# Sliding attention and squared-ReLU MLP, gated: the first tile of tokens in one transfer, four token tiles in turn, warm-up products on the program's constant zero

## The chip, the cores and the metric

The kernel runs on one core of one Trainium2 chip. The core has a matrix engine (TensorE, PE in the profile; its loads of the stationary operand are listed apart as PEld), a vector engine (VectorE, DVE), a scalar engine (ScalarE, ACT), GpSimd (POOL) and a queue engine (SyncE, SP) from which this kernel issues all its transfers. Times are device microseconds of one execution. The metric is the median over several executions; lower is better.

## The reference, cut to what matters

Two branches read the same 2048 tokens of width 448 and are mixed by a gate per token.

```python
g = sigmoid((x * gate_w).sum(-1, keepdims=True))
# branch a: q, k, v for 16 heads of 28; each token sees 8 keys, 2 apart, behind it
qkv = x @ wqkv                                   # 448 -> 3*448
logits = einsum("bhsd,bhswd->bhsw", q, k[idx]) * 28 ** -0.5   # idx = pos - 2*(0..7), masked below 0
o = einsum("bhsw,bhswd->bhsd", softmax(logits), v[idx])
a = o.reshape(1, 2048, 448) @ wo
# branch b: MLP with a squared ReLU
h = relu(x @ w1 + b1) ** 2                       # 448 -> 1792
b = h @ w2 + b2
out = g * a + (1 - g) * b
```

Everything is float32. The kernel splits each operand of a product into a high part in a 32-bit format that TensorE takes at full pace, and a low part, which is the rest. Three products, high by high, high by low and low by high, then stand for one float32 product.

## The kernel before, in words

The tokens lie in four chunks of 512 columns, each of four tiles of 128 tokens; even tokens are in the first two chunks, odd ones in the last two. The width of 448 is cut into three blocks of 128 rows and a last one of 64. These blocks are called k = 0, 1, 2, 3 below, and the last is kept twice, in both halves of the partitions, so that two products of 64 rows run side by side.

The order of the work on every engine is written out by hand. A running estimate of TensorE's time, `advance`, only decides when an operation of another engine is emitted in between; `at` and `when` hang such operations onto that clock. An engine takes its instructions strictly in the order in which they were emitted.

The phases on TensorE are: warm-up products (line 632), which multiply zeros and whose results nobody reads; the query, key and value products of chunk 0 in `qkv_first`; those of chunks 1 to 3 in `qkv_two`, with the first MLP products mixed in; then the MLP of all four chunks, with the output products of attention between them. Attention itself runs on GpSimd and VectorE beside the MLP, by way of copies in HBM.

The first stretch is the one that concerns us. All transfers are issued from SP, in this order: for each k the weights of the query block (line 639 for k below 3, two issues in line 642 for k = 3), then the block of tokens, `rx` (line 644; in the profile `xraw`), which for k = 0 goes in two transfers of 256 columns each; then the key and value weights (lines 649 and 652), then chunk 1 (line 565). SP's transfers pass through eight semaphores in turn, so that a transfer also waits for the one eight places ahead of it.

For each k below 3, ScalarE makes the high part of the weights (line 655) and of the tokens in two halves (line 662). The very first half, k = 0, is made by VectorE instead (line 660). VectorE then makes the low part of the weights (line 663) and those of the two halves of the tokens (line 665). `split_full` (lines 114 and 115) does the same for k = 3.

`qkv_first` makes four accumulators of queries, one for each token tile. For each k it takes the token tiles 0 and 1 first, with three products each (high by high, low weights, low tokens), in turn between the two tiles, and then tiles 2 and 3 in the same way (line 266). Tiles 0 and 1 lie in the first half of the columns, 2 and 3 in the second half. The side-by-side products of k = 3 and all that follows go through `side_by_side` (line 188).

The warm-up products read `zero`, a tile of 128 x 256 which VectorE clears (line 629); it takes a turn in the ring of four product buffers `pp`. Line 630 clears `none`, one element of `b1z`, which ScalarE reads later. The program also has a constant zero of its own, one column of 128 elements, which GpSimd writes before the engines start on the kernel's own instructions (in the profile `const-float32-0.0`).

Of the kernel before, what the change touches and what calls it, by code (L numbers as in the profile page):

```python
# [7 lines left out]
F32 = mybir.dt.float32  # L8
F32R = mybir.dt.float32r
# [5 lines left out]
P = 128  # L15
# [7 lines left out]
CH = 512  # L23
NQ = D + 2
# [23 lines left out]
LEAD = 5  # L48
DEFER = 2
ORDER = (3, 0, 1, 2)  # L50
WARM = 13
PP_BUFS = 4
ST_BUFS = 3
BT_BUFS = 8
# [3 lines left out]
def gated_mix_kernel(ctx: ExitStack, tc: tile.TileContext, xT, wqkv, w1, w2, wo, b1, b2, out):  # L58
    nc = tc.nc

    def f32(ap):
        return ap.bitcast(F32)
# [31 lines left out]
    prodp = ctx.enter_context(tc.tile_pool(name="prodp", bufs=1))  # L94
# [73 lines left out]
    def block(b):  # L168

        o = (0, NP, NP + D)[b]  # L170
        return slice(o, o + ncols(b))
# [45 lines left out]
    def full(x, acc, tl, b, ks=range(3)):  # L217
        sl, n = slice(tl * P, tl * P + P), block(b)
        r = []
        for k in ks:  # L220
            r += [(acc, x.h[k][:, sl], wqh[:, k, n]), (acc, x.h[k][:, sl], wql[:, k, n]),
                  (acc, x.l[k][:, sl], wqh[:, k, n])]
        return r
# [33 lines left out]
    def qkv_first(x):  # L257


        four = range(4)  # L260
        q = accs(0, 0, four, "bbbb")
        for k in range(3):
            for two in ((0, 1), (2, 3)):
                for j, prods in enumerate(zip(*(full(x, q[i], i, 0, (k,)) for i in two))):
                    for acc, a, w in prods:
                        nc.tensor.matmul(acc.pt[:, :NQ], a, w, start=k == j == 0, stop=False)  # L266
            advance(12 * MM448)
        for acc in q:
            acc.todo = 3
        k = accs(0, 1, four, "mmmm")  # L270
        t = [sum((last(x, a[i], i, b) for i in four), []) for b, a in ((0, q), (1, k))]
        f = [full(x, k[i], i, 1) for i in four]
        run(0, [t[0] + f[0] + f[1] + f[2] + f[3], t[1] + f[2] + f[3] + f[0] + f[1]],
            [(3, [(0, 0, q[0])], (k[0], k[0])),
             (12, [(0, i, q[i]) for i in (1, 2, 3)], (k[1], k[1])),
             (24, [], (k[0], k[2])), (33, [], (k[1], k[3])),
             (39, [(1, 0, k[0]), (1, 2, k[2])]), (48, [(1, 1, k[1]), (1, 3, k[3])])])
        v = accs(0, 2, four, "bbbb")
        f, l = [full(x, v[i], i, 2) for i in four], [last(x, v[i], i, 2) for i in four]
        run(0, [f[0] + l[0] + f[2] + l[2] + f[1] + f[3], f[1] + l[1] + f[3] + l[3] + f[0] + f[2]],  # L280
            [(15, [], (v[0], v[1])), (24, [], (v[2], v[3])),
             (33, [(2, 0, v[0]), (2, 1, v[1])]), (42, [(2, 2, v[2]), (2, 3, v[3])])])
# [342 lines left out]


    warm = ps("m", "warm")
    zero = prodp.tile([P, 2 * P], F32R, tag="pp", name="zero", bufs=PP_BUFS)
    nc.vector.memset(f32(zero), 0.0)  # L629
    nc.vector.memset(none, 0.0)  # L630
    for _ in range(WARM):
        nc.tensor.matmul(warm[:, :2 * P], zero[:, :P], zero, start=True, stop=True)  # L632
# [3 lines left out]
    rx = raw_tile("xraw0")  # L636
    for k in range(4):
        if k < 3:
            nc.sync.dma_start(raws[0][:, k, :NQ], wqkv[0, :, k])
        else:  # L640
            for b, rows in ((0, slice(0, 64)), (1, slice(64, P))):
                nc.sync.dma_start(raws[0][rows, k, :NQ], wqkv[b, rows, k])
        for cols in ((slice(0, 256), slice(256, CH)) if k == 0 else (slice(0, CH),)):
            nc.sync.dma_start(rx[:, k, cols], xT[0, :, k, cols])

    for b, tag in ((1, "k"), (2, "v")):
        raw = attp.tile([P, 3, D], F32, tag=tag, name=f"wqraw{b}")
# [5 lines left out]
    x = x_tiles(0, xap)  # L653
# [93 lines left out]
    for c in range(4):  # L747
        x = xs[c]
# [291 lines left out]
    c, x = ORDER[0], xm[3]  # L1040
# [8 lines left out]
    for g in range(2, 2 * NF):  # L1049
        i, f = g // (NF // 2), g % (NF // 2) * 2  # L1050
# [4 lines left out]
        if not f:  # L1055
            x, slots = X([nxt[j][0] for j in range(4)]), [nxt[j][1] for j in range(4)]
# [113 lines left out]
```

## Time and profile before

| | us |
|---|---|
| median of 3 runs | 415.18 |
| lowest and highest run | 414.21, 415.46 |
| the profiled execution | 414.58 |
| its span, first to last instruction | 412.7 |
| TensorE busy (share of the span) | 408.4 (99%) |
| GpSimd busy | 268.6 (65%) |
| VectorE busy | 255.9 (62%) |
| ScalarE busy | 211.9 (51%) |
| DMA of SP's queue, share of 16 engines' span | 54.5% |

The profile is that of one execution. Its rows give the start of a group in microseconds from the start of the span, the time from its first start to its last end, the engine, the line of the kernel, the operation, what it writes and reads, and how many instructions are merged; in brackets stands the idle time before it and what ended that. A row of SPq is the issuing of a transfer and not the transfer itself. Matrix products are pipelined: one product's row is longer than the distance to the next one's start, so that the distance between starts is what tells the pace.

### The profile page before, as it was taken

What the parts mean: (1) busy time and instruction counts of PE and PEld (TensorE: products, weight loads), DVE (VectorE), ACT (ScalarE), POOL (GpSimd) and SP (SyncE); (2) the same over time, 40 slices, a digit from 0 to 9 for tenths busy, and PEclk for the clock granted to TensorE, in tenths of its full rate; (3) what the DMA queues carried; (4) which work ended last, traced back from release to release, by engine and by line L of the source; (5) the groups of instructions that cost most, each with busy time, mean ns of one, the idle gap of its engine ahead of it and who ended that gap; (6) DMA issues with size and microseconds to landing.
All of it is one profiled execution on the core that took longest, in us unless ns stands there. A gap on an engine that the chain in (4) does not pass through costs nothing.

```text
span 412.7 us, 9323 instructions
## 1 busy us (share of the span) xinstructions
PE 408.4 (99%) x3835; PEld 377.6 (91%) x3835; DVE 255.9 (62%) x404; ACT 211.9 (51%) x477; POOL 268.6 (65%) x167
## 2 busy tenths in 40 slices
PE   8999999999999999999999999999999999999997
PEld 8999999999999999888888888989898888888996
DVE  4520523276767767777656798879576677892354
ACT  5642556378756565444565535444653254346540
POOL 0000000965989999999989899999899977860000
PEclk9999999999999999999999999999999999999999
DMA  7989799989164307654112649765145611168204
GB/s 236 380 318 326 227 364 292 363 259 321 47 224 159 128 2 258 207 186 152 37 50 93 233 157 266 200 149 149 24 163 192 224 46 59 72 175 139 91 0 180
DMA packets 65611, 73.76 MB, mean 179 GB/s; under 512 B 32352, under 2 KB 58528, under 8 KB 65184
## 3 DMA queue, kind: packets, MB, share of 16 engines
q1 hardware_dynamic: 65568, 73.16, 54.5%
q8 instruction: 30, 0.49, 0.5%
q14 instruction: 13, 0.11, 0.1%
HBM read 45.71 MB, written 28.25 MB: 179 GB/s over the span
## 4 chain that ended last, share of the span: by engine, by line
PE 99%; DVE 0%; issue 0%
PE b L188 33%; PE h L188 32%; PE qkv L188 23%; PE a L188 7%; PE qkv L266 2%; PE warm L632 1%; PE a L944 1%; PE last L944 0%; DVE bt L823 0%; PE last L936 0%; PE a L936 0%; DVE zero L629 0%; DVE b1z L630 0%
## 5 line engine op out<-in xcount | busy, mean ns | idle before, releaser
L339 POOL TENSOR_TENSOR qk<-q,k 128x896 f32<-128x896 f32 x64 | 135.0, 2138 | 83.2 <-DMA k<-k_d 78.9
L346 POOL TENSOR_TENSOR av<-lg,v 128x896 f32<-128x896 f32 x64 | 119.5, 1962 | 8.0 <-DVE lg L340 5.6
L188 PE MATMUL qkv<-wqh,x 64*128 64x448 f32 (+1 forms) x528 | 90.9, 360 | 0.0
L619 DVE TENSOR_TENSOR h<-h,h 128x512 fp32r<-128x512 f32 x56 | 38.3, 687 | 60.8 <-ACT h L622 60.4
L188 PEld LDWEIGHTS qkv<-wqh,x 64*128 64x128 f32 x528 | 74.0, 184 | 1.3
L188 PE MATMUL qkv<-wql,x 64*128 64x448 f32 (+1 forms) x264 | 74.7, 360 | 0.0
L188 PE MATMUL b<-w2ah,h 64*128 64x448 f32 x448 | 70.4, 359 | 0.0
L188 PE MATMUL b<-w2bh,h 64*128 64x448 f32 x448 | 69.6, 360 | 0.0
L340 DVE TENSOR_REDUCE lg<-qk 128x32 f32<-128x896 f32 x64 | 67.1, 1076 | 2.2 <-POOL qk L339 2.1
L354 DVE TENSOR_REDUCE o<-av 128x112 f32<-128x896 f32 x64 | 66.5, 1070 | 2.1 <-POOL av L346 1.8
L620 ACT ACTIVATE h<-h,b1z 128x512 f32<-128x512 f32 x56 | 36.7, 656 | 44.0 <-PE h L188 44.0
L188 PEld LDWEIGHTS b<-w2ah,h 64*128 64x128 f32 x448 | 48.0, 184 | 2.8
L188 PEld LDWEIGHTS b<-w2bh,h 64*128 64x128 f32 x448 | 46.0, 184 | 3.2 <-ACT h L571 0.3
L188 PE MATMUL b<-w2al,h 64*128 64x448 f32 x224 | 47.6, 358 | 0.0
L188 PEld LDWEIGHTS qkv<-wql,x 64*128 64x128 f32 x264 | 45.5, 184 | 0.7
L188 PE MATMUL b<-w2bl,h 64*128 64x448 f32 x224 | 45.8, 358 | 0.0
L207 ACT ACTIVATE st<-qkv 128x448 f32<-128x448 f32 x48 | 24.5, 543 | 32.2 <-PE qkv L188 27.1
L188 PE MATMUL h<-x,w1h 64*128 64x512 f32 x168 | 36.1, 386 | 0.0
L621 ACT ACTIVATE h<-h 128x512 fp32r<-128x512 f32 x56 | 33.5, 599 | 1.7
L622 ACT ACTIVATE h<-h 128x512 f32<-128x512 f32 x56 | 33.2, 593 | 0.0
L188 PE MATMUL h<-x,w1l 64*128 64x512 f32 x84 | 29.7, 386 | 0.0
L571 ACT ACTIVATE h<-h 128x4 fp32r<-128x4 f32 (+1 forms) x35 | 7.2, 206 | 42.6 <-PE b L188 42.4
(145 smaller groups left out, 749.4 us busy)
## 6 DMA issues: line engine op xcount, KB each, us to landing
k<-k_d SPq DMA_DIRECT2D x8, 840.0 KB, 6.7
v<-v_d SPq DMA_DIRECT2D x8, 840.0 KB, 4.4
x_d<-x SPq DMA_DIRECT2D x11, 512.0 KB, 6.0
q_d<-st SPq DMA_DIRECT2D x8, 448.0 KB, 4.6
k_d<-st SPq DMA_DIRECT2D x8, 448.0 KB, 4.1
v_d<-st SPq DMA_DIRECT2D x8, 448.0 KB, 7.1
w1raw<-w SPq DMA_DIRECT2D x4, 896.0 KB, 10.0
q<-q_d SPq DMA_DIRECT2D x8, 448.0 KB, 3.6
```

Of the source, the lines that this page charges most:

```text
L188: nc.tensor.matmul(acc.pt[:, :acc.n], a[rows], w[rows], start=acc.todo == acc.all, stop=acc.todo == 1)
L207: nc.scalar.activation(st[:, :, t % 2], pt[:, :D].rearrange("p (g c) -> p g c", g=G), AF.Copy)
L266: nc.tensor.matmul(acc.pt[:, :NQ], a, w, start=k == j == 0, stop=False)
L339: nc.gpsimd.tensor_mul(pr, q[:, s:s + 1].to_broadcast([P, W, C]), k[:, s:s + W])
L340: pending.append(lambda: nc.vector.tensor_reduce(lg[:, s], pr.rearrange("p w (h d) -> p w h d", h=HG), axis=AX.X, op=ALU.add))
L346: nc.gpsimd.tensor_mul(pr.rearrange("p (h d) w -> p w h d", h=HG), lg[:, s][:, :, :, None].to_broadcast([P, W, HG, DH]), v[:, s:s + W].rea ...
L354: nc.vector.tensor_reduce(o[:, g * C:(g + 1) * C], pr, axis=AX.X, op=ALU.add)
L571: nc.scalar.activation(ap, f32(ap), AF.Copy)
L619: nc.vector.tensor_sub(hl, pt, f32(hh))
L620: ops += [lambda pt=pt, r=r: nc.scalar.activation(pt, pt, AF.Relu, bias=b1t[:, f + r:f + r + 1]), lambda pt=pt, hh=hh: nc.scalar.activatio ...
L621: lambda pt=pt, hh=hh: nc.scalar.activation(hh, pt, AF.Square),
L622: lambda pt=pt, r=r, low=low: (nc.scalar.activation(pt, pt, AF.Square), at(delays[r], low))]
```

## The change

Four edits. The warm-up products read the program's constant zero, one column repeated 128 and 256 times, and the tile `zero` with its clearing is gone. There are 16 of them where there were 13. The first block of tokens (k = 0) is loaded by one transfer of 512 columns instead of two of 256. `qkv_first` takes all four token tiles in turn for each kind of product: four times high by high, four times low weights, four times low tokens. The splitting of the tokens on ScalarE and VectorE still goes by halves, and nothing else in the program is reordered.

```diff
-WARM = 13
+WARM = 16
@@ qkv_first
         for k in range(3):
-            for two in ((0, 1), (2, 3)):
-                for j, prods in enumerate(zip(*(full(x, q[i], i, 0, (k,)) for i in two))):
-                    for acc, a, w in prods:
-                        nc.tensor.matmul(acc.pt[:, :NQ], a, w, start=k == j == 0, stop=False)
+            for j, prods in enumerate(zip(*(full(x, q[i], i, 0, (k,)) for i in four))):
+                for acc, a, w in prods:
+                    nc.tensor.matmul(acc.pt[:, :NQ], a, w, start=k == j == 0, stop=False)
             advance(12 * MM448)
@@ warm-up
-    zero = prodp.tile([P, 2 * P], F32R, tag="pp", name="zero", bufs=PP_BUFS)
-    nc.vector.memset(f32(zero), 0.0)
+    zero = nc.const_aps.tensor(0.0, [P, 2 * P], F32).bitcast(F32R)
     nc.vector.memset(none, 0.0)
     for _ in range(WARM):
         nc.tensor.matmul(warm[:, :2 * P], zero[:, :P], zero, start=True, stop=True)
@@ first loads
-        for cols in ((slice(0, 256), slice(256, CH)) if k == 0 else (slice(0, CH),)):
-            nc.sync.dma_start(rx[:, k, cols], xT[0, :, k, cols])
+        nc.sync.dma_start(rx[:, k], xT[0, :, k])
```

## The prediction

> **What bounds the kernel now.** I read the page's busy shares, slices and chain first, then the busy time by stretch, then the waits of TensorE, then the timeline of the first 13 us.
>
> ```profile
> PE 408.4 (99%) x3835; PEld 377.6 (91%) x3835; DVE 255.9 (62%) x404; ACT 211.9 (51%) x477; POOL 268.6 (65%) x167
> PE   8999999999999999999999999999999999999997
> PEclk9999999999999999999999999999999999999999
> PE 99%; DVE 0%; issue 0%
> ```
>
> TensorE is busy for 99% of the span and the chain that ended last runs on it for 99%. The next view is the busy time of each engine in four stretches (start:end, length, then PE, PEld, DVE, ACT, POOL, clock, DMA share, GB/s).
>
> ```profile
> 0.00:13.00 13.00, 11.80 (x53) 10.83 (x54) 7.42 (x17) 7.57 (x14) 0.81 (x13) 1.00 0.81 267
> 13.00:100.00 87.00, 87.00 (x866) 84.93 (x864) 31.73 (x97) 49.31 (x118) 19.25 (x10) 1.00 0.93 316
> 100.00:405.00 305.00, 305.00 (x2894) 277.84 (x2892) 213.83 (x287) 154.99 (x346) 248.50 (x145) 1.00 0.43 136
> 405.00:412.70 7.70, 4.62 (x34) 4.02 (x30) 2.91 (x6) 0.00 (x0) 0.00 (x0) 1.00 0.51 184
> ```
>
> From 13 to 405 us TensorE shows 392.00 us busy of 392.00. No wait there can absorb a shift of the first stretch, and none shows that could be shortened. The edit touches the first stretch alone, and what moves the end of that stretch moves the end of the kernel one for one. TensorE has one long wait, at the very start:
>
> ```profile
> PE warm L632 <- DVE b1z L630: 1.2, 1, 1.2
> ```
>
> **The first 13 us.** The timeline (start, length, engine, line, operation, count):
>
> ```profile
> 0.24 0.10 POOL L1162 MEMSET const-float32-0.0<- 128x1 f32 x1 [0.24 <-issue]
> 0.74 1.28 ACT L655 ACT_TABLE_LOAD   x1 [0.74 <-PEq L1162]
> 0.75 0.39 SPq L639 DMA_DIRECT2D wqraw<-wqkv  x1
> 0.87 0.27 DVE L629 MEMSET zero<- 128x256 f32 x1 [0.87 <-PEq L1162]
> 1.08 0.06 DVE L630 MEMSET b1z<- 1x1 f32 x1
> 1.20 3.14 PE L632 MATMUL warm<-zero 128*128 128x256 f32 x13 [1.20 <-DVE b1z L630]
> 1.20 0.89 SPq L644 DMA_DIRECT2D xraw<-xT  x2
> 2.13 0.43 SPq L639 DMA_DIRECT2D wqraw<-wqkv  x1
> 4.13 1.03 PE L266 MATMUL qkv<-wqh,x 128*128 128x450 f32 x2
> 4.96 0.95 PE L266 MATMUL qkv<-wql,x 128*128 128x450 f32 x2
> 5.71 1.44 PE L266 MATMUL qkv<-wqh,x 128*128 128x450 f32 x4
> 6.99 0.57 PE L266 MATMUL qkv<-wql,x 128*128 128x450 f32 x2
> 7.39 0.96 PE L266 MATMUL qkv<-wqh,x 128*128 128x450 f32 x4
> 12.20 0.56 PE L266 MATMUL qkv<-wqh,x 128*128 128x450 f32 x2
> 12.69 0.47 PE L188 MATMUL qkv<-w7h,x 64*128 64x450 f32 x2
> ```
>
> The starts, not the lengths, give the pace. A product of L266 comes every (5.71 - 4.96)/2 = 0.375 us at first, and from 7.39 to 12.20 every 4.81/24 = 0.200 us. TensorE runs at about half speed until somewhere in the group at 5.71, although the granted clock reads full in every slice. Of that group's four, taking 6.99 - 5.71 = 1.28 us, a at 0.375 and 4 - a at 0.200 give a = 2.74: the clock opened at 5.71 + 2.74 x 0.375 = **6.74**, which is 5.54 us after the first warm-up product.
>
> So the stretch has three numbers: S, the start of the first real product (4.13); g, the opening (6.74); and 36 products of L266. The first costs 0.08 extra (0.83 us for two, against 0.75). Then (6.74 - 4.21)/0.375 = 6.75 products run slowly and 29.25 x 0.200 = 5.85 us follow, to 12.59; 0.10 more goes at the switch to L188 at 12.69. A microsecond on S costs 0.200/0.375 = 0.53 us at the end, one on g costs 0.47.
>
> The data that these products need:
>
> ```profile
> 3.34 0.58 ACT L655 ACTIVATE wqh<-wqraw 128x450 fp32r<-128x450 f32 x1 [1.31 <-DMA wqraw<-wqkv]
> 3.64 0.29 DVE L660 CAST x<-xraw 128x256 fp32r<-128x256 f32 x1 [2.50 <-DMA xraw<-xT]
> 3.95 0.63 DVE L663 TENSOR_TENSOR wql<-wqraw,wqh 128x450 fp32r<-128x450 f32 x1
> 4.49 0.42 DVE L665 TENSOR_TENSOR x<-xraw,x 128x256 fp32r<-128x256 f32 x1
> 5.54 0.42 ACT L662 ACTIVATE x<-xraw 128x256 fp32r<-128x256 f32 x1 [1.63 <-DMA xraw<-xT]
> 6.18 0.58 ACT L655 ACTIVATE wqh<-wqraw 128x450 fp32r<-128x450 f32 x1 [0.23 <-DMA wqraw<-wqkv]
> 6.93 0.72 ACT L662 ACTIVATE x<-xraw 128x256 fp32r<-128x256 f32 x2 [0.17 <-DMA xraw<-xT]
> 8.86 0.72 ACT L662 ACTIVATE x<-xraw 128x256 fp32r<-128x256 f32 x2 [0.73 <-DMA xraw<-xT]
> 2.00:3.00 1.00, 1.00 (x6) 1.00 (x6) 0.00 (x0) 0.03 (x1) 0.00 (x0) 1.00 0.84 284
> ```
>
> **The change, part by part.**
>
> *Warm-up operand.* The clear of 0.27 us on DVE goes, and with it TensorE's wait for DVE. The constant zero is written at 0.24 to 0.34, ahead of the first instruction of every queue at about 0.74. TensorE can start between 0.74 (ACT) and 0.87 (DVE); I take the middle, 0.80, a gain of 0.40 us. At worst it stays at 1.20. The clear of b1z stays on DVE, with nothing in front; its reader is ten microseconds away. A ring of four product buffers loses one early owner, POOL's first product comes late in the 13 to 100 stretch: nothing.
>
> *Sixteen warm-ups.* Thirteen took 4.13 - 1.20 = 2.93 us, 0.225 each; sixteen take 3.61. They end at 0.80 + 3.61 = **4.41** instead of 4.13, which costs 0.28 on S if the data are there earlier. That a column read over and over goes at the pace of a tile is not shown; the nearest rows are these thirteen products, and I take their pace.
>
> *One transfer for the first x tile.* L644 issues two for it now, in 0.89 us. One goes, so the queue behind it (weights of the second tile, then x, and so on) moves up by about 0.44 us, the third transfer from 2.13 to about 1.69. Further back the six issues of L649 take 3.76 us, 0.63 each, since a transfer waits there for the one eight places ahead of it; with one fewer ahead that wait ends no later.
>
> ```profile
> 5.90 3.76 SPq L649 DMA_DIRECT2D wqraw<-wqkv  x6
> ```
>
> In return the DVE cast at 3.64, which needed 128 KB, now needs 256 KB. Bounds of the landing: 3.64 (the extra half is free) and 5.54 (when ACT took up the second half). The extra 128 KB at the 284 GB/s of the slice from 2 to 3 take 0.46 us, so **4.10**; I stay near the lower end since the gap to 5.54 belongs to a transfer issued a place later. Behind the cast on DVE wait the subtractions of L663 and L665, each 0.46 later: wql is ready at 4.10 + 0.29 + 0.63 = 5.02, the low parts of x at 5.44 and 5.86. ACT takes the second half of x at 4.10 rather than 5.54, and is done at 4.52.
>
> The first real product then waits for the cast: 4.10 + 0.29, and 0.06 from DVE to TensorE as at 1.14 to 1.20, makes **S = 4.45**. TensorE idles 0.04 us. At most S is 5.54 + 0.29 + 0.06 = 5.89.
>
> *Four token tiles in turn.* Same 36 products. The third now needs the second half of x, at 4.45 + 0.08 + 0.75 = 5.28 against 4.52: covered by 0.76 us. With the landing of before it would have waited until 5.96. The fifth needs wql at 6.03 against 5.02, the ninth the low parts at about 7 against 5.86. The thirteenth falls near 7.8 and needs the weights and x of the second tile, ready now at 6.76 and 7.65, and 0.44 earlier after the change; the twenty-fifth falls near 10.2 against 9.58. All are covered.
>
> *The opening.* I let it follow TensorE's first product, as the one opening shown allows: g = 6.74 - 0.40 = **6.34**. If it doesn't move, 6.74.
>
> *Sum.* (6.34 - 4.53)/0.375 = 4.83 slow products; the other 31.17 take 6.23; end at 12.57, with 0.10 for the switch 12.67, against 12.69: **-0.02 us**. With g at 6.74 it is 5.89 slow ones, 12.86, +0.17. Span 412.7 and 1.9 us around it make the profiled 414.58; after, 414.56. That execution lies 0.6 below the median of the runs, 415.18; the runs spread over 1.25 us. The mean of the four executions known (414.21, 414.58, 415.18, 415.46) is 414.86, and 414.86 - 0.02 = **414.8** is my number. The spread itself is 0.3%, which is about what a measurement can tell. As no other stretch has any slack, I suspect it is the opening that varies: 1.25/0.47 = 2.7 us of g.
>
> The Trainium skill (TensorE: Matmul & The Clock Gate, Part 1: The HAM clock gate) says that a free-running window of about 3.4 us releases the clock after sustained work, and that time, not the number of products, is what counts. That speaks against the three extra products as such; here the trace shows an opening later than one such window and earlier than two.
>
> **The rivals.**
>
> *The clock opens early (0.13).* With the opening 4.0 us after the first product, g = 4.80: 0.72 slow products, 35.28 x 0.200 = 7.06, end 11.96, so -0.73: 413.85 against the profiled time, 414.1 against the mean. At best g precedes S: 4.53 + 7.20 + 0.10 = 11.83, -0.86. The feed allows it: the thirteenth product at 6.9 finds its x at 6.93 - 0.44 + 0.41 = 6.90. Against it: the one opening shown took 5.54 us. For it: the spread of the runs. The same page and section of the Trainium skill puts the transition around 4 us, give or take half a microsecond, which is this rival; the 5.54 us here disagree with it.
>
> *The whole transfer lands late (0.15, the one on the slower side).* If 256 KB land only at 5.54, S = 5.89 and TensorE idles 1.47 us. With g at 6.74: 2.05 slow products, 33.95 x 0.200 = 6.79, end 13.63, **+0.94**: 415.8 against the mean. It is slower by over 0.3% (1.25 us) once the idle stretch also puts the opening past 6.74 + 0.31/0.47 = 7.40; if the 5.54 us count anew from 5.89, g = 11.43, and +3.1 results, 418. For it: the second half did land 1.9 us after the first. Against it: its place in the queue was a later one.
>
> *The warm-ups don't start earlier (0.12).* If TensorE is held to 1.20 by something the trace doesn't name, sixteen end at 4.81: 4.93 slow products, 31.07 x 0.200 = 6.21, end 13.05, +0.36: 415.2. The change is then a small loss by its own extra products. Against it: the wait's releaser is DVE.
>
> **How the numbers follow.** The forecast, within about 0.3 us of no change, has 0.60. It and the third rival stay inside 0.3%; the early opening reaches -0.86 and passes 1.25 only with the scatter of a few executions; of the late landing rather more than half passes. Faster 0.11, same 0.80, slower 0.09. The range goes from the early opening at 413.9 to the late landing at 415.9.
>
> **What would show it.** Warm-up row: 16 products, starting near 0.80, waiting for no DVE. First L266 row near 4.45, with the DVE cast just before it and starting near 4.10; the ACT copy of the second half right beside it and not at 5.54. The pace of L266 changing from 0.375 to 0.200 near 6.3. First L188 row near 12.7, everything behind it shifted alike. The prediction is wrong if TensorE idles between warm-up and L266, if the warm-ups keep another pace, if the opening moves by more than half a microsecond either way, or if some wait after 13 us appears.

## The result and the profile after

| | before | after |
|---|---|---|
| median of six executions, us | 414.24 | 417.21 |
| lowest and highest, us | 414.11, 415.46 | 416.09, 418.09 |
| the profiled execution, us | 414.58 | 416.09 |
| its span, us | 412.7 | 414.3 |

The changed kernel takes 1.0061 times as long as the one before (95% interval 1.005 to 1.0073): about 2.5 us more (the two medians lie 2.97 us apart). The profiled execution is the fastest of its six, so its trace shows less than the usual loss. A second profile of the same kernel, among the experiments, shows the usual one.

The page of the changed kernel names a transfer in the chain that ended last, which was not there before:

```profile
span 414.3 us, 9325 instructions
...
PE 98%; DMA 1%; DVE 0%; ACT 0%; SPq 0%; issue 0%
```

TensorE's waits have changed places. The wait for VectorE ahead of the warm-up is gone; what is left there is the start at 0.78, close to that of the other engines. A longer one stands ahead of the first real product (microseconds in total, times, longest):

```profile
PE qkv L265 <- ACT x L659: 1.7, 1, 1.7
PE warm L630 <- PEq L1159: 0.8, 1, 0.8
```

The timeline of the first 14 us (line 630 was 632 before, 641 was 644, 657 was 660, 659 was 662, 265 was 266):

```profile
0.78 3.75 PE L630 MATMUL warm<-const-float32-0.0 128*128 128x256 f32 x16 [0.78 <-PEq L1159]
...
1.20 0.42 SPq L641 DMA_DIRECT2D xraw<-xT  x1
...
1.66 0.43 SPq L637 DMA_DIRECT2D wqraw<-wqkv  x1
...
3.48 0.58 ACT L652 ACTIVATE wqh<-wqraw 128x450 fp32r<-128x450 f32 x1 [1.46 <-DMA wqraw<-wqkv]
...
5.76 0.42 ACT L659 ACTIVATE x<-xraw 128x256 fp32r<-128x256 f32 x1 [1.70 <-DMA xraw<-xT]
5.76 0.29 DVE L657 CAST x<-xraw 128x256 fp32r<-128x256 f32 x1 [4.90 <-DMA xraw<-xT]
...
6.20 1.06 PE L265 MATMUL qkv<-wqh,x 128*128 128x450 f32 x4 [1.66 <-ACT x L659]
...
7.09 0.99 PE L265 MATMUL qkv<-wql,x 128*128 128x450 f32 x4
...
8.47 0.72 ACT L659 ACTIVATE x<-xraw 128x256 fp32r<-128x256 f32 x2 [1.52 <-DMA xraw<-xT]
...
8.94 0.70 PEld L265 LDWEIGHTS qkv<-wqh,x 128*128 128x128 f32 x4 [0.41 <-ACT x L659]
...
13.94 0.47 PE L188 MATMUL qkv<-w7h,x 64*128 64x450 f32 x2
```

The warm-up starts at 0.78, and sixteen products are through at about 4.5. The weights are in ScalarE's hands at 3.48. The tokens, issued at 1.20, come at 5.76. TensorE stands idle for 1.66 us, and the first product starts at 6.20 where it started at 4.13. The second block of tokens is late as well (8.47 against 6.93 before), although it was issued earlier. The first product of L188 starts at 13.94, that is 1.25 us later than before.

In this execution the clock was already open when the real products began: (7.09 - 6.20) / 4 = 0.22 us each. The trace file also keeps a record of the granted clock, which no view prints (the views read 1.00 from the start). Its first entry at full clock is at 5.11, against 6.70 before, where the prediction had worked out 6.74 from the pace. With a later opening the loss would, by the prediction's own sum, have been larger.

What the transfers did meanwhile, by stretches of one microsecond (start:end, length, PE, PEld, DVE, ACT, POOL, clock, DMA share, GB/s), in the changed kernel:

```profile
2.00:3.00 1.00, 1.00 (x6) 1.00 (x6) 0.00 (x0) 0.02 (x1) 0.00 (x0) 1.00 0.88 289
3.00:4.00 1.00, 1.00 (x7) 1.00 (x6) 0.00 (x0) 0.52 (x1) 0.00 (x0) 1.00 0.88 120
4.00:5.00 1.00, 0.54 (x3) 0.24 (x2) 0.00 (x0) 0.06 (x1) 0.00 (x0) 1.00 0.72 137
5.00:6.00 1.00, 0.00 (x0) 0.00 (x0) 0.24 (x2) 0.24 (x1) 0.00 (x0) 1.00 0.88 304
```

and in the kernel before:

```profile
3.00:4.00 1.00, 1.00 (x7) 1.00 (x5) 0.34 (x2) 0.58 (x1) 0.00 (x0) 1.00 0.44 112
4.00:5.00 1.00, 1.00 (x5) 0.87 (x5) 0.91 (x2) 0.00 (x0) 0.00 (x0) 1.00 0.90 258
```

The last two columns have to be read together. Between 3 and 4 us both kernels move little, but before, the DMA engines were idle for half of the time (0.44), and after, they are busy (0.88) at 120 GB/s: their packets are slow. The trace file's record of single packets, which no view lists either, shows it directly. A packet of 2048 B, one row of a block of tokens, usually takes 84 ns; of the first 128 of them to start in the changed kernel, 30 took more than twice that, the longest 952 ns. The slow spell lasts a microsecond longer than the lull before.

### The profile page after: what moved, and what is told of

The parts are those of the page before. It is cut to its first block, busy times and chain, and to the rows that moved or that the text cites. A ratio compares the mean times of both kernels' runs of the same rounds, so it can differ in the third digit from the quotient of the medians.

```text
span 414.3 us, 9325 instructions
## 1 busy us (share of the span) xinstructions
PE 408.7 (99%) x3838; PEld 377.2 (91%) x3838; DVE 255.4 (62%) x403; ACT 212.1 (51%) x477; POOL 268.4 (65%) x167
## 4 chain that ended last, share of the span: by engine, by line
PE 98%; DMA 1%; DVE 0%; ACT 0%; SPq 0%; issue 0%
PE b L188 33%; PE h L188 32%; PE qkv L188 23%; PE a L188 7%; PE qkv L265 2%; DMA xraw<-xT 1%; PE a L941 1%; PE last L941 0%; DVE bt L820 0%; ACT x L659 0%; SPq L637 0%; PE last L933 0%; PE a L933 0%
## 5 line engine op out<-in xcount | busy, mean ns | idle before, releaser
L188 PE MATMUL qkv<-wqh,x 64*128 64x448 f32 (+1 forms) x528 | 90.9, 360 | 0.0
L188 PEld LDWEIGHTS qkv<-wqh,x 64*128 64x128 f32 x528 | 74.1, 184 | 1.3
L188 PE MATMUL qkv<-wql,x 64*128 64x448 f32 (+1 forms) x264 | 74.7, 360 | 0.0
L188 PE MATMUL b<-w2ah,h 64*128 64x448 f32 x448 | 70.4, 359 | 0.0
L188 PE MATMUL b<-w2bh,h 64*128 64x448 f32 x448 | 69.7, 360 | 0.0
L188 PEld LDWEIGHTS b<-w2ah,h 64*128 64x128 f32 x448 | 48.1, 184 | 2.8
L188 PEld LDWEIGHTS b<-w2bh,h 64*128 64x128 f32 x448 | 46.1, 184 | 3.6 <-DVE h L618 0.4
L188 PE MATMUL b<-w2al,h 64*128 64x448 f32 x224 | 47.6, 358 | 0.0
L188 PEld LDWEIGHTS qkv<-wql,x 64*128 64x128 f32 x264 | 45.5, 184 | 0.7
L188 PE MATMUL b<-w2bl,h 64*128 64x448 f32 x224 | 45.8, 358 | 0.0
L188 PE MATMUL h<-x,w1h 64*128 64x512 f32 x168 | 36.1, 386 | 0.0
L188 PE MATMUL h<-x,w1l 64*128 64x512 f32 x84 | 29.7, 386 | 0.0
```

What stands on the lines that cost most here:

```text
L188: nc.tensor.matmul(acc.pt[:, :acc.n], a[rows], w[rows], start=acc.todo == acc.all, stop=acc.todo == 1)
```

## The experiments

The questions were, in this order: which of the four edits costs the time; why the one transfer lands late; and why most executions lose more than the profiled one. Each kernel was timed against the one before on its own chip. "Landing" is the start of VectorE's cast, which waits for the tokens; "S" the first real product; "L188" the first product of that line; "opening" the first entry at full clock in the trace file's record.

| kernel | median, us | ratio to before (95%) | landing | S | opening | L188 |
|---|---|---|---|---|---|---|
| before | 414.24 | 1 | 3.64 (half) | 4.13 | 6.70 | 12.69 |
| after | 417.21 | 1.0061 (1.005 to 1.0073) | 5.76 | 6.20 | 5.11 | 13.94 |
| after_again | 416.96 | 1.0059 (1.0045 to 1.0073) | 5.16 | 5.61 | 8.74 | 14.44 |
| merge_only | 416.19 | 1.0045 (1.0031 to 1.0059) | 5.67 | 6.11 | 4.60 | 13.57 |
| warm_only | 414.70 | 1.0003 (0.9994 to 1.0012) | 3.79 (half) | 4.33 | 6.90 | 12.85 |
| halves | 414.97 | 1.0021 (1.0008 to 1.0034) | 3.70 (half) | 4.33 | 4.81 | 12.97 |
| two_by_two | 415.94 | 1.0038 (1.0024 to 1.0051) | 5.49 | 5.93 | 4.25 | 13.62 |
| x_first | 415.54 | 1.0021 (0.9999 to 1.0043) | 4.74 | 6.11 | 5.26 | 13.55 |
| x_act | 416.74 | 1.0029 (1.0007 to 1.0052) | 5.46 | 5.92 | 10.31 | 15.38 |
| x_contig | 415.23 | 1.0004 (0.9988 to 1.002) | 4.16 | 4.60 | 4.26 | 12.39 |
| bridge | 416.25 | 1.0023 (1.0007 to 1.0038) | 5.76 | 6.20 | 4.04 | 14.07 |
| x_pad | 416.14 | 1.004 (1.0026 to 1.0053) | 4.01 | 4.45 | 5.21 | 13.51 |
| four_blocks | 414.62 | 1.0005 (0.9996 to 1.0014) | 4.05 | 4.49 | 5.67 | 12.52 |
| best | 414.39 | 0.9998 (0.9989 to 1.0007) | 3.60 (half) | 4.04 | 5.24 | 12.23 |
| pad_all | 414.64 | 0.9992 (0.9977 to 1.0006) | 4.00 | 4.45 | 3.62 | 12.58 |
| copy_8k | 416.67 | 1.0051 (1.0035 to 1.0068) | 5.11 | 5.55 | 4.84 | 13.98 |

The first four experiments shared one chip, as did x_first, x_act, x_contig and bridge; after_again, x_pad, four_blocks and best; and the last pair. The kernel before had a median of 414.44, 414.8, 414.38 and 414.62 in these groups, so ratios are compared, not times. On the second of these chips six of the 35 executions of the kernel before took 416.40 to 418.17 us, which lowers the ratios there: the medians alone would give 1.0018 for x_first, 1.0047 for x_act, 1.0010 for x_contig and 1.0035 for bridge. In the kernels with copied tokens (`x0`) the first 512 tokens are given once more, as an input of their own in another layout.

### Which edit: the transfer alone

In the kernel before, only the transfer is merged:

```diff
-        for cols in ((slice(0, 256), slice(256, CH)) if k == 0 else (slice(0, CH),)):
-            nc.sync.dma_start(rx[:, k, cols], xT[0, :, k, cols])
+        nc.sync.dma_start(rx[:, k], xT[0, :, k])
```

> The kernel before with the one transfer of 512 columns alone (13 warm-up products on the cleared tile, token tiles two by two). Landing theory: the loss sits in this edit; the first tile of tokens lands near 5.7 us as in the changed kernel's profile, TensorE idles from about 4.1 to 6.2, and the kernel loses most of the 3 us between the medians, +1.5 to +3 us (ratio 1.004 to 1.007). Order theory (taking four tiles in turn makes the third product wait): this kernel keeps the old order, so no loss, within 0.3 us. Warm-up theory (the earlier and longer warm-up, or its operand, delays the opening of the clock): no loss either.

Its timeline:

```profile
5.67 0.30 DVE L659 CAST x<-xraw 128x256 fp32r<-128x256 f32 x1 [4.53 <-DMA xraw<-xT]
...
6.11 0.65 PE L266 MATMUL qkv<-wqh,x 128*128 128x450 f32 x2 [1.77 <-ACT x L661]
```

1.0045: three quarters of the loss with this edit alone. The landing is at 5.67 and TensorE idles for 1.77 us.

### Which edit: the warm-up alone

In the kernel before, only the constant zero and the 16 products:

```diff
-WARM = 13
+WARM = 16
...
-    zero = prodp.tile([P, 2 * P], F32R, tag="pp", name="zero", bufs=PP_BUFS)
-    nc.vector.memset(f32(zero), 0.0)
+    zero = nc.const_aps.tensor(0.0, [P, 2 * P], F32).bitcast(F32R)
```

> The kernel before with the warm-up edits alone: constant zero, 16 products. Landing theory: warm-ups from 0.8 to 4.4, first real product at about 4.4 with its data there since 3.9, so between -0.2 and +0.2 us, ratio 0.9995 to 1.0005. Warm-up theory: the loss is here, +1 us or more (ratio above 1.0025), with the clock opening later than 6.7.

```profile
0.78 3.75 PE L631 MATMUL warm<-const-float32-0.0 128*128 128x256 f32 x16 [0.78 <-PEq L1161]
...
4.33 0.99 PE L266 MATMUL qkv<-wqh,x 128*128 128x450 f32 x2
```

1.0003: no difference to be measured. The warm-up starts 0.42 us earlier and, with three products more, hands over 0.20 us later (4.33 against 4.13). The column that is read again and again goes at the pace of the tile: (4.33 - 0.78) / 16 = 0.222 us for each product, against 0.225 before.

### Which edit: the order with the halves kept

The changed kernel with the two transfers of 256 columns put back:

```diff
-        nc.sync.dma_start(rx[:, k], xT[0, :, k])
+        for cols in ((slice(0, 256), slice(256, CH)) if k == 0 else (slice(0, CH),)):
+            nc.sync.dma_start(rx[:, k, cols], xT[0, :, k, cols])
```

> The changed kernel with the first tile of tokens in two transfers again; constant zero, 16 products and four tiles in turn stay. Landing theory: the first half lands near 3.6 again, so the first product starts at 4.4; the third waits for the second half (5.5 + 0.42) at about 6.0 instead of 5.3, 0.7 us of idling, and the kernel comes within +0.2 to +0.8 us of before, 414.4 to 415.0. Order theory: most of the loss stays, 416 or more. Warm-up theory: the same.

```profile
5.49 0.42 ACT L660 ACTIVATE x<-xraw 128x256 fp32r<-128x256 f32 x1 [1.51 <-DMA xraw<-xT]
...
5.96 0.68 PE L265 MATMUL qkv<-wqh,x 128*128 128x450 f32 x2 [0.84 <-ACT x L660]
```

Two thirds of the loss go (1.0021 from 1.0061). What is left is seen in the rows: with four tiles in turn the third product needs the second half of the tokens, which comes at 5.49, and TensorE waits for it until 5.96. So the order costs 0.84 us of idleness with halves; whether any of that shows in the time against warm_only (1.0003) is at the edge of the intervals. Nine of its twelve executions took 414.70 to 415.30 us and three 416.60 to 417.27; the profiled one, 415.02, is of the nine.

### Which edit: one transfer, the order put back

```diff
-            for j, prods in enumerate(zip(*(full(x, q[i], i, 0, (k,)) for i in four))):
-                for acc, a, w in prods:
+            for two in ((0, 1), (2, 3)):
+                for j, prods in enumerate(zip(*(full(x, q[i], i, 0, (k,)) for i in two))):
+                    for acc, a, w in prods:
```

> The changed kernel with the old order of the products (tiles 0 and 1, then 2 and 3); one transfer, constant zero and 16 products stay. Landing theory: the same loss as the changed kernel, 416.5 to 417.5, with the first product near 6.2, or a little more, since the low weights are needed two products earlier while VectorE makes them only after the cast. Order theory: the loss goes, 414.0 to 414.6.

1.0038, and landing and S are late here too (5.49, 5.93). With the tokens whole, the order of the products cannot be told from the other one: the intervals just touch (1.0051 above here, 1.005 below with the change). The median of 415.94 is below the 416.5 that the landing theory expected. The merged transfer is the edit that costs most.

### Why late: the place in the queue

The tokens' transfer is issued first, ahead of the weights:

```diff
+    nc.sync.dma_start(rx[:, 0], xT[0, :, 0])
     for k in range(4):
...
-        nc.sync.dma_start(rx[:, k], xT[0, :, k])
+        if k:
+            nc.sync.dma_start(rx[:, k], xT[0, :, k])
```

> The changed kernel with the first tile of tokens issued ahead of the first weights instead of behind them; everything else as changed. Every profile so far has a lull of the transfers from about 3.1 us on (112 to 150 GB/s from 3 to 4). Lull theory: whatever is complete by then lands in time, whatever is not lands past 5. Then the tokens land at about 3.4 and the weights, second in the queue, take their place and land near 5.0 to 5.5; the first product moves by little, 5.8 to 6.2, and the loss stays, 416 to 417.3. Slow tokens theory (the transfer of 2048-byte rows is itself the slow one): the tokens land past 4.5 though they are first; the first product is no later than in the changed kernel.

```profile
4.74 0.29 DVE L659 CAST x<-xraw 128x256 fp32r<-128x256 f32 x1 [3.87 <-DMA xraw<-xT]
...
5.48 0.58 ACT L654 ACTIVATE wqh<-wqraw 128x450 fp32r<-128x450 f32 x1 [3.46 <-DMA wqraw<-wqkv]
```

and its busy time by stretches:

```profile
2.00:3.00 1.00, 1.00 (x6) 1.00 (x6) 0.00 (x0) 0.03 (x1) 0.00 (x0) 1.00 0.57 154
```

With nothing ahead of it the tokens still take until 4.74, and the weights, now behind them, come at 5.48 rather than 3.48. The slow spell has moved forward with the transfer: 154 GB/s already from 2 to 3 us, where the change had 289. It is the tokens' transfer that is slow, wherever it stands. The first product starts at 6.11, hardly earlier than in the changed kernel; the ratio, 1.0021, has an interval that reaches no change.

### Why late: the issuing engine

The tokens' transfer is issued by ScalarE, beside SP:

```diff
-        nc.sync.dma_start(rx[:, k], xT[0, :, k])
+        (nc.scalar if k == 0 else nc.sync).dma_start(rx[:, k], xT[0, :, k])
```

> The changed kernel with the first tile of tokens issued from ScalarE's queue at about 0.75 us, beside the weights from SP. Lull theory with a lull in time or in bytes: 480 KB are asked for at once, at 285 GB/s they need until about 3.4, so both land just at the edge of the lull: tokens between 3.6 and 5.5, the gain uncertain. If the lull belongs to SP's queue of transfers (their issue or their descriptors): no lull for the tokens, landing at 3.3 to 3.8, first product at 4.2 to 4.5, the kernel at 414.2 to 414.8, the loss gone. Slow tokens theory: landing stays past 5, loss stays.

```profile
5.29 0.58 ACT L652 ACTIVATE wqh<-wqraw 128x450 fp32r<-128x450 f32 x1 [2.83 <-DMA wqraw<-wqkv]
...
5.46 0.29 DVE L657 CAST x<-xraw 128x256 fp32r<-128x256 f32 x1 [4.61 <-DMA xraw<-xT]
...
7.59 1.70 PE L265 MATMUL qkv<-wql,x 128*128 128x450 f32 x4
...
9.09 2.37 PE L265 MATMUL qkv<-wqh,x 128*128 128x450 f32 x8
```

Now both are late, 5.29 and 5.46. Another issuing engine does not mend it. The Trainium skill (DMA: Bandwidth & Descriptors, Issuing engines are not separate DMA queues) says that transfers of all issuing engines interleave on the same DMA engines, so that a second issuer saves only issue time; these rows agree.

This trace shows a second thing. The products come every (9.09 - 7.59) / 4 = 0.375 us, the slow pace, more than 3 us after the first at 5.92; the clock's record has the opening at 10.31. L188 starts at 15.38, the latest of all. It comes back below.

### Why late: rows side by side

`xT` lies in memory as 128 rows for each chunk; a row holds its four blocks of 512 tokens one behind the other, 4 x 2048 B. One block is therefore 128 rows of 2048 B that begin 8192 B apart. Here a copy of the first block lies with its rows side by side:

```diff
-        nc.sync.dma_start(rx[:, k], xT[0, :, k])
+        nc.sync.dma_start(rx[:, k], x0 if k == 0 else xT[0, :, k])
...
+        "x0": ktiles(xp[0])[:, 0],
```

> The changed kernel with the first tile of tokens read from a copy of its own in HBM, 256 KB in one piece, instead of 128 rows 8 KB apart; the copy is an input. Slow tokens theory, with the rows 8 KB apart as cause: landing near 3.9 to 4.2, first product at 4.4, loss gone (414.2 to 414.8). Lull theory: landing stays at 5 or later, since the lull is not a matter of the address; loss stays at 416 to 417.3.

```profile
4.16 0.29 DVE L657 CAST x<-xraw 128x256 fp32r<-128x256 f32 x1 [3.30 <-DMA xraw<-x]
...
12.39 0.47 PE L188 MATMUL qkv<-w7h,x 64*128 64x450 f32 x2
...
85.38 0.58 ACT L515 ACTIVATE w1h<-w1raw 128x448 fp32r<-128x448 f32 x1 [1.53 <-DMA w1raw<-w]
```

The landing falls to 4.16, and most of the loss goes with it (1.0004, by the medians 1.0010; the median of 415.23 lies above the 414.2 to 414.8 that were expected). L188 starts 0.30 us earlier than in the kernel before, yet the span is 413.9. TensorE's waits say where that went:

```profile
PE qkv L188 <- DVE qkv L198: 1.1, 1, 1.1
```

Just before 89.7 us TensorE waits 1.1 us for VectorE, which comes after weights that landed late (the row at 85.38). In the stretch of dense transfers from 13 to 100 us a gain at the start can be lost again.

### Why late: the distance of the rows

"Side by side" changes two things: the distance of the rows, and that the copy is a tensor of its own. The next copy has rows apart, but padded to 8704 B:

```diff
-        nc.sync.dma_start(rx[:, k], xT[0, :, k])
+        nc.sync.dma_start(rx[:, k], x0[:, k * CH:k * CH + CH] if k == 0 else xT[0, :, k])
...
+        "x0": _np.pad(ktiles(xp[0]).reshape(P, 4 * CH), ((0, 0), (0, 128))),
```

> The changed kernel with the first tile of tokens read from a copy in HBM whose rows of 2048 bytes lie 8704 bytes apart instead of 8192; still 128 separate rows. With 256 KB in one piece the tokens landed at 4.2. Power-of-two theory (rows exactly 8 KB apart collide in HBM): landing near 4.0 to 4.3 here too, first product near 4.6, median near that of the contiguous copy, within 0.2% of before. Separate-rows theory (rows apart are slow by themselves): landing stays past 5, loss stays at 1.5 us or more.

```profile
4.01 0.29 DVE L657 CAST x<-xraw 128x256 fp32r<-128x256 f32 x1 [3.15 <-DMA xraw<-x]
...
8.03 0.72 ACT L659 ACTIVATE x<-xraw 128x256 fp32r<-128x256 f32 x2 [0.90 <-DMA xraw<-xT]
...
8.50 1.09 PE L265 MATMUL qkv<-wqh,x 128*128 128x450 f32 x4 [1.04 <-ACT x L659]
```

The first block lands at 4.01, earlier than any whole block with 8192 B. But the second block still comes from `xT`, lands at 8.03, and TensorE waits 1.04 us for it. The loss has only moved on by one block (1.004). That is not the distance alone: in x_contig the second block comes from `xT` too and lands at 6.91. Why it is late here and not there is open.

So all four blocks were taken from copies, first each block side by side:

```diff
-        nc.sync.dma_start(rx[:, k], xT[0, :, k])
+        nc.sync.dma_start(rx[:, k], x0[k])
...
+        "x0": ktiles(xp[0]).transpose(1, 0, 2),
```

> The changed kernel with all four blocks of the first chunk of tokens read from contiguous copies. If the rows 8 KB apart are the cause of the slow stretch: no lull after 3 us in any transfer of the first chunk (over 250 GB/s from 2 to 9), tokens at 4.1, first product at 4.5 to 4.6, the second block's tokens before 6.5; ratio to before 0.997 to 1.000. If not: as the changed kernel, 1.004 to 1.007.

Its busy time by stretches:

```profile
3.00:4.00 1.00, 1.00 (x7) 1.00 (x6) 0.00 (x0) 0.58 (x1) 0.00 (x0) 1.00 0.99 333
```

333 GB/s from 3 to 4 us instead of 120, landing at 4.05, ratio 1.0005: the loss is gone. Two details of the expectation did not come true: the second block lands at 7.03, not before 6.5, and the rate falls below 250 GB/s again, to 240 from 7 to 8 us.

The last pair differs in the padding alone. `pad_all` reads all four blocks from a copy with rows 8704 B apart, `copy_8k` from a copy with rows 8192 B apart, as in `xT`:

```diff
-        nc.sync.dma_start(rx[:, k], xT[0, :, k])
+        nc.sync.dma_start(rx[:, k], x0[:, k * CH:k * CH + CH])
...
+        "x0": _np.pad(ktiles(xp[0]).reshape(P, 4 * CH), ((0, 0), (0, 128))),   # pad_all
+        "x0": ktiles(xp[0]).reshape(P, 4 * CH),                                # copy_8k
```

> The changed kernel with all four token blocks of the first chunk read from a copy in HBM whose rows lie 8704 bytes apart; 128 separate rows of 2048 bytes per transfer as in the changed kernel. If the 8192 bytes between rows are the cause: tokens land at 4.0, those of the second block before 7, no wait of TensorE after the warm-up, and the median within 0.15% of before, as with contiguous copies. If contiguity counts: the second block lands near 8 again as with the padded first block alone, and the kernel stays 1.5 us or more slower.

> The same with a copy whose rows lie exactly 8192 bytes apart, so that only the distance between rows differs from the padded copy, and only the tensor from the changed kernel. If the distance is the cause: as the changed kernel, tokens past 5, first product past 5.5, 416.5 to 417.3. If a copy of its own is what helped (an own place in HBM): as the padded one, 414.3 to 415.

The timeline of pad_all:

```profile
4.00 0.29 DVE L657 CAST x<-xraw 128x256 fp32r<-128x256 f32 x1 [3.14 <-DMA xraw<-x]
...
4.45 1.06 PE L265 MATMUL qkv<-wqh,x 128*128 128x450 f32 x4 [0.28 <-ACT x L659]
```

its stretch from 3 to 4 us:

```profile
3.00:4.00 1.00, 1.00 (x8) 0.97 (x6) 0.00 (x0) 0.58 (x1) 0.00 (x0) 1.00 1.05 303
```

the timeline of copy_8k:

```profile
5.11 0.29 DVE L657 CAST x<-xraw 128x256 fp32r<-128x256 f32 x1 [4.25 <-DMA xraw<-x]
...
5.55 1.06 PE L265 MATMUL qkv<-wqh,x 128*128 128x450 f32 x4 [1.02 <-ACT x L659]
```

and its stretch:

```profile
3.00:4.00 1.00, 1.00 (x7) 1.00 (x6) 0.00 (x0) 0.55 (x1) 0.00 (x0) 1.00 0.71 171
```

Same program, same bytes in the same number of rows of 2048 B, one chip: with 8704 B between rows the tokens land at 4.00 and the ratio is 0.9992 (0.9977 to 1.0006); with 8192 B they land at 5.11 and it is 1.0051 (1.0035 to 1.0068). The packets show the same. Of the first 128 packets of 2048 B in the order of their starts, none of the second 64 took more than 84 ns in pad_all; in copy_8k eight of these 64 took more than twice that, up to 655 ns. The distance of the rows is the cause of the late first block and of the loss. That the rows are not side by side, or that the copy is a tensor of its own, is not. No distance other than these two was tried. The second block of pad_all lands at 7.11, where less than 7 was expected, and TensorE waits 0.42 us for it.

### Why most executions lose more: the clock

The changed kernel once more, for a second profile:

> The changed kernel itself, a second profile of it. Its first profile is the fastest of its six runs and shows the clock open at 5.1 us, before the first real product at 6.2. Two-part theory (the late landing puts the first product at 6.2, and in most executions the idle stretch of 1.7 us before it also makes the clock open late): an execution of 417 or more shows 0.375 us between products for several microseconds after 6.2, an opening past 7; one near 416 shows none. If the median's further 1 us is something else, an execution of 417 shows products at 0.200 from the start and a wait further back, such as TensorE waiting near 88 us.

```profile
5.61 1.84 PE L265 MATMUL qkv<-wqh,x 128*128 128x450 f32 x4 [1.06 <-ACT x L659]
...
7.24 1.67 PE L265 MATMUL qkv<-wql,x 128*128 128x450 f32 x4
...
8.74 1.77 PE L265 MATMUL qkv<-wqh,x 128*128 128x450 f32 x8
...
10.35 0.96 PE L265 MATMUL qkv<-wql,x 128*128 128x450 f32 x4
...
14.44 0.47 PE L188 MATMUL qkv<-w7h,x 64*128 64x450 f32 x2
```

The tokens land earlier here (5.16 against 5.76), the first product starts at 5.61 rather than 6.20, and yet L188 starts later, 14.44 against 13.94. From 7.24 to 8.74 four products take 1.50 us, 0.375 each; from 8.74 on eight take 1.61, 0.20 each. The clock opened only at 8.74. This execution took 417.20 us, the one with the opening at 5.11 took 416.09. Of the 2.7 us that its span is longer than that of the kernel before, 1.75 lie ahead of L188. Of the other 0.95 TensorE's waits show a part, which the list of the kernel before does not have:

```profile
PE b L188 <- DVE h L618: 0.6, 1, 0.6
```

It is a wait at 364 us, far back. Why VectorE is late there was not tried.

Two more profiles point the same way, each of a single execution. The ten executions of x_act fall into two groups, 414.98 to 415.14 and 416.40 to 418.11; the profiled one, with the opening at 10.31, took 417.23. Those of x_first fall into 415.23 to 415.56 and 416.96 to 417.59; the profiled one, with the opening at 5.26, took 415.38. S is nearly the same in the two profiles (5.92 and 6.11); L188 differs by 1.83 us and the times by 1.85.

If idleness ahead of the first product makes a late opening likely, then more warm-up products should help though they bring the data no earlier. The changed kernel with 24:

```diff
-WARM = 16
+WARM = 24
```

> The changed kernel with 24 warm-up products instead of 16, so that TensorE has no idle stretch of 1.7 us between the warm-up (which ends at 4.5) and the first product at 6.2. If the idle stretch also puts the opening of the clock off in most executions (the runs of the changed kernel lie 1 us above its profiled one, which opened at 5.1): the opening comes by 5 to 6.7 in all, and the median falls to 415.4 to 416.1. If landing alone matters and the opening is not put off: no change from the changed kernel, 417.0 to 417.3, or later where the warm-ups run past the landing.

```profile
0.79 4.47 PE L630 MATMUL warm<-const-float32-0.0 128*128 128x256 f32 x24 [0.79 <-PEq L1159]
...
6.20 1.06 PE L265 MATMUL qkv<-wqh,x 128*128 128x450 f32 x4 [0.95 <-ACT x L659]
```

S is the same 6.20 as with 16, the idle time 0.95 instead of 1.66 us, and the ratio falls to 1.0023 (1.0007 to 1.0038), below both intervals of the changed kernel (1.0045 and up). By the medians it is 1.0035, the changed kernel was not timed beside it, and the median of 416.25 is a little above the 415.4 to 416.1 that were expected. None of its twelve executions took more than 416.74; five of the first six of the changed kernel took 417.07 or more, and the four of after_again 416.65 to 417.20. So more warm-up products took away about half of the loss.

That they do it through the clock is argued and not shown. The one profile of bridge has its opening early, at 4.04, and yet this execution took 416.72, one of the longest of its twelve. Half a microsecond of that is a wait as in x_contig, which ends at 90.72 and stands behind weights that landed late:

```profile
PE qkv L188 <- DVE qkv L198: 0.5, 1, 0.5
```

Nor does a long execution need idleness ahead of the first product: the kernel before has none, and six of its 35 executions on this chip took 416.40 us or more. None of those was traced. So one part of the loss is what the late data cost by themselves; another goes with a late opening in the two executions where one was seen (8.74 and 10.31). What puts the opening back is open.

### A version from what was found

In the kernel before, the warm-up reads the constant zero, 14 products, and the halves are read from the copies of four_blocks, whose rows of 2048 B lie side by side, so that the rows of a half, 1024 B each, begin 2048 B apart; the order of the products is that of before:

```diff
-WARM = 13
+WARM = 14
...
-            nc.sync.dma_start(rx[:, k, cols], xT[0, :, k, cols])
+            nc.sync.dma_start(rx[:, k, cols], x0[k, :, cols])
...
```

> The kernel before (two transfers for the first block, token tiles two by two) with the constant zero, 14 warm-up products and the first chunk's tokens from contiguous copies. Warm-ups from 0.79 to 4.0, first half of the tokens at 3.6, first product at 4.0 to 4.1 instead of 4.14, no wait after it: 0.05 us by the earlier start and, on average, 0.2 us by the earlier activity; ratio 0.998 to 1.000. A stall near 88 us, where the weights of the MLP land late, would hide it.

```profile
4.04 1.09 PE L266 MATMUL qkv<-wqh,x 128*128 128x450 f32 x2
...
12.23 0.47 PE L188 MATMUL qkv<-w7h,x 64*128 64x450 f32 x2
```

L188 starts 0.46 us earlier than before and the profiled span is 412.2, the shortest of all; the ratio, 0.9998 (0.9989 to 1.0007), cannot be told from no change. No version beat the kernel before by more than its measurement can tell.

## Why the prediction was wrong

**What bounds the kernel: right in the main.** TensorE stays 98% of the chain, and what moves L188 moves the end: of the 1.6 us by which the profiled span grew, 1.25 lie ahead of L188. "Moves the end of the kernel one for one" was too strong: 0.35 us here, 0.95 in the second profile, 0.85 in bridge and 1.4 in x_contig came on top further back.

**Warm-up operand and sixteen products: right.** Start at 0.78 (said 0.80), no wait for VectorE, the next product at 4.33 (4.41) in warm_only, which has these two edits alone and shows no difference in time.

**The one transfer: the step that failed.** "The extra 128 KB at the 284 GB/s of the slice from 2 to 3 take 0.46 us, so 4.10". This landing is the term of the sum that was mis-sized, and S came out 1.75 us late with it. The tokens landed at 5.76, and at 5.16 in the second profile. The rate was taken from a microsecond that was over before the bytes in question were due. The next slice, 3 to 4 us, had 112 GB/s in the kernel before; at that the 131 KB take 1.17 us, which would have given 4.81 and the warning, though no price, since that low rate came with engines that stood idle (0.44) and not with slow packets. The reason for choosing the low end, that the second half came late because it was "issued a place later", was half of the story: in `best`, with rows side by side, the second half still lands at 5.01 where the whole block of four_blocks lands at 4.05, so the second place does cost; but with 8192 B between rows the whole block lands as late as the second half did. With that distance taken away the step holds to 0.10 us: pad_all lands at 4.00. That its first product starts at 4.45, exactly the S that was predicted, is luck, since the landing was put 0.10 us too late and the step from there to the product 0.10 us too short.

**S from the landing: right, 0.1 us short.** The first product follows ScalarE's half of the tokens rather than VectorE's cast: 5.76 + 0.42 + 0.02 = 6.20, where the prediction's 0.29 + 0.06 give 6.11.

**Later blocks 0.44 earlier: wrong.** They were issued earlier (the weights of the second tile at 1.66), but the second block of tokens landed at 8.47 instead of 6.93. That the slow transfer ahead of it holds it up is argued; the distance of its own rows does not suffice, since x_contig has the same rows there and lands them at 6.91. "With one fewer ahead that wait ends no later" was wrong too. The six issues that wait for transfers eight places ahead now take 5.29 us instead of 3.76, and end at 11.04 instead of 9.66:

```profile
5.75 5.29 SPq L646 DMA_DIRECT2D wqraw<-wqkv  x6
```

**Four in turn: right on the waits.** "With the landing of before it would have waited until 5.96": in halves the third product started at 5.96. With the block whole no wait of its own shows. Whether the order costs time is not settled: halves is slower than warm_only (1.0021 and 1.0003), and the changed kernel than two_by_two (1.0061 and 1.0038), both by about 0.2%, but the intervals overlap each time.

**The opening: wrong.** It was to follow TensorE's first product by 5.54 us. By the clock's record it came between 2.83 and 6.12 us after the first warm-up product in fourteen of the sixteen profiles, and 7.95 and 9.53 us after it in the other two, after_again and x_act, both with more than a microsecond of idle time ahead of the real products (five others with 1.02 to 1.77 us of idle time there, that of the change among them, have it at 3.41 to 4.47). What the prediction suspected, that the opening is what varies from one execution to the next, is part of the truth: waits near 90 and 364 us vary too. Its formula holds: for the second profile (8.74 - 5.69) / 0.375 = 8.13 slow products and 27.87 x 0.200 = 5.57 us give 14.31, with 0.10 for the switch 14.41, against 14.44. For the first, with the opening ahead of S, 6.20 + 0.08 + 7.20 + 0.10 = 13.58, and about 0.3 for the wait at 8.94 for the second block makes 13.88, against 13.94.

**The rivals.** The late landing, given 0.15 and the slower side, is what happened. Its condition for a loss over 0.3%, an opening past 7.40, held in the second profile (8.74) but not in the first, which lost 1.51 us, 0.36%, with an opening at 5.11. Its two prices, +0.94 and +3.1 us, have the measured loss of about 2.5 us between them. The early opening came true as well, in the profiled execution, and hid part of the loss there. The median of 417.21 lies above the range, whose upper end of 415.9 priced the late landing without the late opening.

## What to carry to other kernels

An added transfer is not safely priced by the rate of an earlier microsecond: here the rate fell from 289 to 120 GB/s just as the bytes in question were due. Read the DMA share beside the GB/s. In this kernel a low share with a low rate (0.44 at 112) meant engines that stood idle, and a high share with a low rate (0.88 at 120) meant slow packets. Where the first loads of a kernel gate its first product, look at the distance between the rows that a transfer reads; padding rows from 8192 to 8704 B was worth 1.1 us of landing time here. And let the warm-up products reach up to the first data: eight more of them took about half of the loss away here, for a reason that is not fully shown.

## What the runs showed of the hardware that was not expected

**The distance of the rows.** 128 rows of 2048 B, 8192 B apart, issued behind one transfer of weights at 1.20 us, landed between 5.11 and 5.76 us in five kernels of that order of transfers (six profiles); 8704 B apart or side by side they landed at 4.00 to 4.16. Why this distance is slow is not shown, and it is not slow everywhere: the second block, with the same 8192 B, landed at 6.91 in x_contig and at 8.03 in x_pad. Rows of 1024 B at the same distance, the first half in the kernel before, in warm_only and in halves, came in time (3.64 to 3.79). The packets narrow that down. Counted by their starts, the first 64 packets of 2048 B, as many bytes as such a half, were under way by 3.28 us in all ten profiles. Of the next 64, 8 to 27 took more than twice the usual 84 ns in the six profiles with 8192 B; with the other two layouts none took more than 84 ns. So the slow packets are mostly those after the first 131 KB. Why they come only there is open.

**A lull that remains.** The kernel before leaves its DMA engines half idle from 3 to 4 us (0.44), and so does `best` (0.43, 127 GB/s) with rows side by side, while four_blocks has 0.99. So this lull belongs to the halves and not to the distance. It is no lack of issued work: in the kernel before, transfers issued at 2.13 and 2.61 had still not landed at 6 us. Its cause is open.

**The clock.** In the fourteen profiles without a late opening it came 2.83 to 6.12 us after the first warm-up product, a spread of 3.3 us. The Trainium skill (TensorE: Matmul & The Clock Gate, Part 1: The HAM clock gate) speaks of a free-running window of about 3.4 us; the spread agrees with it. The same section puts the transition around 4 us, give or take half a microsecond; that holds for six of the sixteen profiles. That some idle time inside such a window is what put the opening to 7.95 and 9.53 us would fit the gain of bridge, but was not shown for a single execution.

**A constant column.** One column of zeros read 128 and 256 times over goes through TensorE as fast as a tile of zeros (3.75 us for sixteen products, 3.14 for thirteen; 0.222 and 0.225 us from start to start), and saves the clearing.
